# A softcapped attention and mixer kernel: when token weights are decoded, when sums are gathered, and what the start issues first

## The chip, the cores and the metric

The kernel runs on one core of one Trainium2 chip. The metric is device time in microseconds (us) of one execution; below it is called the time. A profiled execution also has a span, from its first to its last instruction.

## The reference

Attention with softcapped scores over 4 batches, 12 heads, 448 positions and 64 columns a head, and then a mixer of two stages with residuals. All is in float32.

```python
scores = (q @ k.T) / sqrt(64)
scores = cap * tanh(scores / cap)
attn = softmax(scores)
x = (attn @ v)                       # heads side by side: 4 x 448 x 768
h = relu(x.T @ w_tok1) @ w_tok2      # over positions: 448 -> 256 -> 448
u = x + h.T
out = u + relu(u @ w_ch1) @ w_ch2    # over columns: 768 -> 1536 -> 768
```

The four weight matrices come as 64-bit floats; the kernel reads their bits and splits each into a high and a low float32 part itself. That is the decode below.

## The kernel before, in words

**Units and steps.** Heads go in pairs (p = 0 to 5 in a batch b), and keys in chunks: three full ones of 128 (c = 0 to 2) and the last 64 keys of two neighbouring pairs packed together (c = 3, which belongs to the even pair). A unit is one (b, p, c). The list of 84 units goes pair 0: c = 0, 1, 2, 3, pair 1: c = 0, 1, 2, pair 2 and so on; a step takes two units, so there are 42 steps (L487), and the units of batch 0 lie in steps 0 to 10.

**What a step does.** A unit's scores are made by `qk_unit` (L173) on TensorE, then `tanh_unit` (L190) and `exp_unit` (L195) on ScalarE write a tile `e`. Step t first multiplies step t's exp tiles with V on TensorE (`pv_full`, `pv_packed`), then calls `scores_of(t + 2)` (L470), which makes scores, tanh and exp two steps ahead and, when a pair's last scores are made, loads the pair three ahead. Then VectorE adds up the exp tiles of step t (`add_up`, L229; `add_packed`, L249), which later gives the softmax's row sums. At the end, `background` (L413) fills TensorE with work of the token mixer that is ready, up to a budget in ns: transposes (L320), `tok1` (L341), `tok2` (L363) and `add_rows` (L256).

**Buffers.** There are 8 tiles `e` (L191); a tile comes free when its PV products and its additions are done. There are two banks for scores (`ps_a`), two for PV outputs (`ps_b`), and two for everything else (`ps_c`). A pair's PV output stays in its `ps_b` bank until `evac` (L274) copies it out on VectorE, which is put at the head of the step after the pair's last product. Pair 2's output is finished in step 5 and copied at the head of step 6; the first product of pair 4 (step 7) takes its bank. Pairs' raw Q and K have three buffers, decode inputs (`wraw`) and decode work tiles (`wz`) two each.

**The order.** The whole attention part is in an order written out by hand (L449): each of the five engines, SP's queue of DMA issues among them, runs its instructions in the order in which the program emits them. `at(d, f, y)` (L71) puts f off by d steps into phase y: phase 0 at the head of a step, before its PV products, phase 1 after `scores_of`, before the additions, phase 2 after `background`, at the end.

**The decode.** `decode` (L88) issues the load of one piece on SP, and then makes seven operations on VectorE in four parts: `first` (L98, L101), `second` (L106, L107), `third` (L110, L111), `fourth` (L115), with one subtraction on GpSimd at the end (L118). The token weights are four pieces, two of 512 and two of 448 columns. A piece is issued in a step that holds a unit with c = 1 of batch 0: steps 0, 2, 4 and 6. `first` comes two steps later at the head, `second`, `third` and `fourth` three, four and five steps later at the end.

**The normalisation.** After the second pair of two has its last chunk, `add_rows` multiplies the added-up tiles with ones in the next step's background. One step on, `take` (L265) copies the sums out on VectorE in phase 1. One step on, in phase 0, `gather` (L279) issues four small DMAs on SP that bring the sums into one tile of 128 partitions. One step on, in phase 1, `norm` (L286) takes the reciprocal on VectorE and stores it. One step on, `spread` (L293) issues four broadcasting loads, and at the end of the step after that `scale_pair` (L299) multiplies the two outputs. Only scaled pairs are transposed, and `tok1` needs the transposes of three pairs.

**The start.** `load_pair(0, 0)` issues Q on SP (L161) and K on ScalarE's queue (L162); the cap follows K (L453); then come pair 1, V, pair 2 and two more V on SP. From the cap VectorE makes the scales of tanh and exp (L463 to L465).

**After the attention** the channel mixer runs, with `tok` work of the last batches as filling; the change touches there only the moment of the last gathers (`pace` is 2 there).

Of the kernel before, what the change touches and what calls it, by code (L numbers as in the profile page):

```python
# [8 lines left out]
F32 = mybir.dt.float32  # L9
# [6 lines left out]
P = 128  # L16
# [14 lines left out]
HALF = C // 2  # L31
NHALF = NC // 2
SP = 32
FREE = 40.0
EPS = 1e-9


@with_exitstack
def tile_softcap_mixer(ctx, tc, qk, v, cap, w1, w2, wc1, wc2, out):
    nc = tc.nc  # L40
# [5 lines left out]
    ps_c = ctx.enter_context(tc.tile_pool(name="ps_c", bufs=2, space=PSUM))  # L46

    def bits(ap):
        return ap.bitcast(F32)

    cap_sb = const.tile([P, 1], F32, name="cap_sb")
# [19 lines left out]
    def at(d, f, y=0):  # L71
        later.setdefault((now[0] + d, y), []).append(f)

    def run(y):
        for f in later.pop((now[0], y), []):
            f()

    def tick(most=3):
        now[0] += 1
        for y in range(most):  # L80
            run(y)
# [4 lines left out]
    pace = [1]  # L86

    def decode(src, n, hi, lo, early, blank):  # L88
        r = wp.tile([P, 2 * DU], I32, tag="wraw", name="wraw")[:, :2 * n]
        nc.sync.dma_start(r, src.bitcast(I32))  # L90
        r = r.rearrange("p (n t) -> p n t", t=2)

        z = wp.tile([P, DU], I32, tag="wz", name="wz")[:, :n]
        zf = bits(z)

        def first():
            if early:
                nc.vector.tensor_scalar(  # L98
                    z, r[:, :, 1], 1, 1, op0=ALU.logical_shift_left, op1=ALU.logical_shift_right
                )  # L100
                nc.vector.tensor_scalar_mul(zf, zf, 2.0 ** -16)  # L101
                return
            nc.scalar.activation(zf, bits(r[:, :, 1]), AF.Abs, scale=2.0 ** -16)  # L103

        def second():
            nc.vector.tensor_scalar(zf, zf, 2.0 ** -31, 2.0 - 2.0 ** -23, op0=ALU.max, op1=ALU.min)  # L106
            nc.vector.tensor_scalar(z, z, 4, 1, op0=ALU.logical_shift_left, op1=ALU.logical_shift_right)  # L107

        def third():
            nc.vector.scalar_tensor_tensor(z, r[:, :, 1], -(1 << 31), z, op0=ALU.bitwise_and, op1=ALU.bitwise_or)  # L110
            nc.vector.scalar_tensor_tensor(z, r[:, :, 0], 29, z, op0=ALU.logical_shift_right, op1=ALU.bitwise_or)  # L111

        def fourth():
            if early:
                nc.vector.tensor_copy(hi, zf)  # L115
            else:
                nc.scalar.activation(hi, zf, AF.Copy)  # L117
            nc.gpsimd.tensor_tensor(lo, zf, hi, op=ALU.subtract)  # L118
            if blank is not None:
                nc.gpsimd.memset(bits(blank), 0.0)  # L120

        d = lag[0]
        at(d, first)
        d += slow[0]
        at(d, second, 2)
        at(d + 1, third, 2)
        at(d + 2, fourth, 2)

    def decode_steps(src, dst, n, early=False, blank=None):
        hi = dst[:, 0].rearrange("p a b -> p (a b)")  # L130
        lo = dst[:, 1].rearrange("p a b -> p (a b)")
        return [
            lambda i=i: decode(
                src[:, i:i + n], n, hi[:, i:i + n], lo[:, i:i + n], early, blank if i + n == hi.shape[1] else None
            )
            for i in range(0, hi.shape[1], n)
        ]
# [20 lines left out]
    def load_pair(b, p):  # L158
        raw = pi.tile([P, 2, S], F32, tag="qkraw", name="qkraw", bufs=3)
        if b == 0 and p == 0:  # L160
            nc.sync.dma_start(raw[:, 0], qk[b, p, :, 0])  # L161
            nc.scalar.dma_start(raw[:, 1], qk[b, p, :, 1])  # L162
        else:
            nc.sync.dma_start(raw, qk[b, p])
        raws[b, p] = raw

    def load_v(b, p):
        nc.sync.dma_start(vn[p % 3], v[b, p])
# [42 lines left out]
    def pv_full(b, p, c):  # L211
        ps, first, last = pv_bank(b, p)
        for j in range(2):
            nc.tensor.matmul(  # L214
                ps[j * D:(j + 1) * D, :S], vn[p % 3][:, j * NF + c], es[b, p, c][:, j], start=first, stop=last
            )

    def pv_packed(b, p):
        for i in range(2):
            ps, first, last = pv_bank(b, p + i)  # L220
            for j in range(2):
                r = half(i, j)
                nc.tensor.matmul(  # L223
                    ps[j * D:(j + 1) * D, :S], vn[(p + i) % 3][r, NV - 1], es[b, p, NF][r, i], start=first, stop=last
                )
# [30 lines left out]
    def add_rows(b, q):  # L256
        ps = ps_c.tile([P, 512], F32, tag="c", name="ps_s")
        acc = accs.pop((b, q))
        for i in range(2):
            for j in range(2):  # L260
                r = (2 * i + j) * SP
                nc.tensor.matmul(ps[r:r + SP, :S], ones, acc[:, i, j], start=True, stop=True, tile_position=(0, r))  # L262
        yield 750, True

        def take():  # L265
            x = px.tile([P, S], F32, tag="xs", name="xs", bufs=1)
            nc.vector.tensor_copy(x, ps[:, :S])
            at(pace[0], lambda: gather(b, q, x))

        read_at(b, None, take)  # L270

# [7 lines left out]
    def gather(b, q, x):  # L279
        s = px.tile([P, S // SP], F32, tag="sums", name="sums", bufs=1)  # L280
        for i in range(4):
            r = slice(i * SP, (i + 1) * SP)
            nc.sync.dma_start(s[r], x[i * SP:i * SP + 1, :].rearrange("p (a c) -> p a c", a=SP))
        at(pace[0], lambda: norm(b, q, s), 1)

    def norm(b, q, s):  # L286
        nc.vector.reciprocal(s, s)
        r = pd.tile([4, S], F32, tag="rs", name="rs")
        nc.sync.dma_start(r.rearrange("h (a c) -> (h a) c", a=SP), s)
        for i in range(2):  # L290
            at(pace[0], lambda i=i: spread(b, 2 * q + i, r[2 * i:2 * i + 2]))
# [104 lines left out]
    second = {}  # L396
# [4 lines left out]
    def read_at(b, f, g):  # L401
        def free():
            unread[0] -= 1
            left[b] -= 1

        if f is not None:
            at(1, f)
        at(1, g, 1)
        at(slack[0], free, 0 if slack[0] > 1 else 1)
# [18 lines left out]
    def split_tile(b, pool):  # L428
        t = last_u if pool is None else pool.tile([P, 2 * NC * S], F32R, name=f"uhl{b}", bufs=1)
        uhl[b] = t.rearrange("p (x c s) -> p x c s", x=2, c=NC)  # L430
# [13 lines left out]
    for m, (b, p, c) in enumerate(units):  # L444
# [5 lines left out]
        engines={engines.PE, engines.DVE, engines.Activation, engines.Pool, engines.SP}  # L450
    ))
    load_pair(*pairs[0])
    nc.scalar.dma_start(cap_sb, cap)  # L453
    nc.vector.memset(near, 0.0)
    nc.scalar.activation(near, near, AF.Exp)
    load_pair(*pairs[1])
# [10 lines left out]
    tokw_steps = decode_steps(w1, w1s, DU, True, w1s[:LAST, 1, NK - 1]) + decode_steps(w2, w2s, S, True)  # L467
# [19 lines left out]
    for t in range(steps_in):  # L487
        two = units[2 * t:2 * t + 2]
        tick(0)
        run(0)  # L490
        for b, p, c in two:
            if c < NF:
                pv_full(b, p, c)
        for b, p, c in two:
            if c == NF:
                pv_packed(b, p)
        scores_of(t + 2)
        run(1)
        for b, p, c in two:
            add_up(b, p, c)  # L500
            n = pairs.index((b, p))
            if c == (2 if p % 2 else NF) and n + 3 < len(pairs):
                at(1, lambda n=n: load_v(*pairs[n + 3]))
            if b == 0 and c == 1 and tokw_steps:
                tokw_steps.pop(0)()
            if b >= 1 and p % 2 and c == 2 and w0_steps:
                w0_steps.pop(0)()
        late = t + 2 - steps_in
        if late >= 0:
            if late == 0:  # L510
                nc.vector.tensor_scalar(
                    mag, cap_sb.bitcast(I32), 1, 1, op0=ALU.logical_shift_left, op1=ALU.logical_shift_right
                )
                in_att.close()
                m0 = ctx.enter_context(tc.tile_pool(name="m0", bufs=1, reuse_waits="tile", side="right"))
                split_tile(0, m0)
            for cc in range(3 * late, 3 * late + 3):
                split_u(0, cc)
        background(TOK / 9)
        run(2)  # L520
        for b, p, c in two:
            if p % NHALF == NHALF - 1 and c == 2:
                work.extend(tok_work(b, p // NHALF))
# [102 lines left out]
    def attend(b, h, vr):  # L626
# [5 lines left out]
        for c in range(NK):  # L632
# [7 lines left out]
            nc.vector.reduce_sum(st[:, 1:2], t, axis=mybir.AxisListType.X)  # L640
            nc.vector.tensor_scalar_add(st[:, 1:2], st[:, 1:2], EPS)
            nc.vector.reciprocal(st[:, 1:2], st[:, 1:2])
# [103 lines left out]
```

## Time and profile before

| | us |
|---|---|
| Runs of the kernel, three | 609.04, 608.09, 607.51 |
| Median of the runs | 608.09 |
| Time of the profiled execution | 606.1 |
| Its span | 604.3 |

The profiled execution is 1.8 us longer than its span: that lies before the first and after the last instruction. Times in the rows below are from the span's start. PE is TensorE's matmul, DVE is VectorE, ACT is ScalarE, POOL is GpSimd, SP is SyncE, and a q behind an engine's name means its queue, which waits or issues a DMA. What stands in square brackets is the idle time of the engine before the row and what ended it. In the rows below L191 and the like are lines of the kernel before.

### The profile page before, as it was taken

How to read it: one execution, taken by the hardware profiler on the slowest of the kernel's cores; microseconds unless marked ns; L12 is line 12 of the kernel's file. 1: busy time of each engine (PE TensorE's matmuls, PEld its weight loads, DVE VectorE, ACT ScalarE, POOL GpSimd, SP SyncE). 2: the span in 40 equal slices, each digit the busy share in tenths (PEclk: the TensorE clock that was granted, in tenths of full speed). 3: DMA queues.
4: the chain of work that ended last, by engine and by line, in shares of the span. 5: the costliest groups of instructions: out<-in, count | busy, mean ns of one | idle time of the engine just before them, and what ended most of it. 6: DMA issues, size and time to landing. Idle time of an engine off the chain costs nothing.

```text
span 604.3 us, 7751 instructions
## 1 busy us (share of the span) xinstructions
PE 590.4 (98%) x3008; PEld 437.3 (72%) x3008; DVE 385.3 (64%) x626; ACT 254.4 (42%) x330; POOL 54.5 (9%) x48
## 2 busy tenths in 40 slices
PE   7998999999999999999999999999999999999997
PEld 2232444444444489997998999899989999999986
DVE  2899869696996996547788386438643853333324
ACT  6998987887879733115332022012211220000000
POOL 0020000000010000002331022001200120000000
PEclk9999999999999999999999999999999999999999
DMA  6445445254442211001344121202120200000224
GB/s 202 149 143 152 143 132 160 78 157 143 130 160 82 68 31 32 0 1 36 96 120 132 36 68 57 86 0 78 63 70 1 69 2 0 1 1 0 94 100 178
DMA packets 24476, 49.12 MB, mean 81 GB/s; under 512 B 6768, under 2 KB 16368, under 8 KB 24432
## 3 DMA queue, kind: packets, MB, share of 16 engines
q1 hardware_dynamic: 24000, 48.21, 24.8%
q8 instruction: 25, 0.41, 0.3%
q10 hardware_dynamic: 432, 0.34, 0.2%
q14 instruction: 19, 0.16, 0.1%
HBM read 42.86 MB, written 5.59 MB: 80 GB/s over the span
## 4 chain that ended last, share of the span: by engine, by line
PE 82%; DVE 10%; ACT 3%; DMA 2%; issue 2%; POOL 0%; DVEq 0%; ACTq 0%; SPq 0%
PE ps_o L563 26%; PE ps_g L546 26%; PE ps_pv L214 8%; PE ps_qk L179 7%; PE ps_h L350 5%; PE ps_u L370 5%; PE ps_s L262 2%; PE ps_pv L223 2%; DMA wraw<-in_wc 1%; DVE wz L110 1%; PE ps_qk L185 1%; PE ps_t L323 1%; ACT e L192 1%; DVE u L568 1%; DVE acc L254 1%
## 5 line engine op out<-in xcount | busy, mean ns | idle before, releaser
L563 PE MATMUL ps_o<-g,wc 128*128 128x448 f32 x864 | 182.8, 367 | 0.2 <-DVE u L568 0.2
L563 PEld LDWEIGHTS ps_o<-g,wc 128*128 128x128 f32 x864 | 161.5, 188 | 15.6 <-DVE u L568 1.3
L546 PE MATMUL ps_g<-uhl,wc 128*128 128x448 f32 x648 | 138.3, 367 | 0.0
L546 PEld LDWEIGHTS ps_g<-uhl,wc 128*128 128x128 f32 x648 | 120.9, 188 | 10.3
L568 DVE TENSOR_TENSOR u<-u,ps_o 128x448 f32<-128x448 f32 (+1 forms) x145 | 86.8, 613 | 47.1 <-PE ps_o L563 46.8
L192 ACT ACTIVATE e<-ps_qk,tsc 128x896 f32<-128x896 f32 x84 | 81.1, 1023 | 28.3 <-PE ps_qk L179 22.3
L197 ACT ACTIVATE e<-e,near 128x896 f32<-128x896 f32 x84 | 83.6, 1059 | 0.0
L118 POOL TENSOR_TENSOR wc<-wz,wc 128x512 fp32r<-128x512 f32 x36 | 48.2, 1342 | 385.6 <-ACT wc L117 364.3
L551 ACT ACTIVATE g<-ps_g 128x896 fp32r<-128x896 f32 x24 | 22.0, 916 | 143.1 <-PE ps_g L546 143.1
L552 DVE SCALAR_TENSOR_TENSOR g<-ps_g,g 128x896 fp32r<-128x896 f32 x24 | 26.1, 1089 | 75.0 <-ACT g L551 75.0
L179 PE MATMUL ps_qk<-qkraw 64*128 64x448 f32 x288 | 67.6, 581 | 4.5 <-DMA qkraw<-in_qk 4.0
L214 PE MATMUL ps_pv<-e,vn 128*64 128x448 f32 x288 | 64.2, 556 | 0.4 <-ACT e L192 0.4
L179 PEld LDWEIGHTS ps_qk<-qkraw 64*128 64x128 f32 x288 | 24.4, 189 | 46.3 <-issue 13.2
L117 ACT ACTIVATE wc<-wz 128x512 fp32r<-128x512 f32 x36 | 22.6, 629 | 74.9 <-PE ps_g L546 33.9
L546 PE MATMUL ps_g<-last_u,wc 128*128 128x448 f32 x216 | 45.5, 367 | 0.7 <-PE ps_o L563 0.6
L546 PEld LDWEIGHTS ps_g<-last_u,wc 128*128 128x128 f32 x216 | 40.4, 188 | 4.8 <-issue 0.9
L103 ACT ACTIVATE wz<-wraw 128x512 f32<-128x512 f32 x36 | 24.2, 673 | 45.8 <-DMA wraw<-in_wc 30.5
L214 PEld LDWEIGHTS ps_pv<-e,vn 128*64 128x64 f32 x288 | 16.5, 135 | 33.3 <-issue 16.0
L106 DVE TENSOR_SCALAR wz<-wz 128x512 f32<-128x512 f32 (+1 forms) x40 | 17.5, 437 | 34.7 <-ACT wz L103 34.6
L350 PEld LDWEIGHTS ps_h<-wc,last_u 128*128 128x128 f32 x176 | 30.5, 188 | 8.0 <-issue 6.0
L350 PE MATMUL ps_h<-wc,last_u 128*128 128x384 f32 x176 | 36.0, 343 | 0.0
L370 PE MATMUL ps_u<-last_u,wc 128*128 128x448 f32 x144 | 34.1, 376 | 1.5 <-DVE wc L359 0.8
(48 smaller groups left out, 410.5 us busy)
## 6 DMA issues: line engine op xcount, KB each, us to landing
wraw<-in_wc SPq DMA_DIRECT2D x36, 512.0 KB, 3.5
qkraw<-in_qk SPq DMA_DIRECT2D x23, 448.0 KB, 3.4
vn<-in_v SPq DMA_DIRECT2D x24, 224.0 KB, 3.3
rb<-rs SPq DMA_DIRECT2D x48, 112.0 KB, 2.8
out_t<-u SPq DMA_DIRECT2D x23, 224.0 KB, 1.9
wraw<-in_w SPq DMA_DIRECT2D x2, 512.0 KB, 4.7
wraw<-in_w SPq DMA_DIRECT2D x2, 448.0 KB, 3.4
sums<-xs SPq DMA_DIRECT2D x48, 1.8 KB, 2.1
```

What stands on the lines that cost most here:

```text
L103: nc.scalar.activation(zf, bits(r[:, :, 1]), AF.Abs, scale=2.0 ** -16)
L118: nc.gpsimd.tensor_tensor(lo, zf, hi, op=ALU.subtract)
L179: nc.tensor.matmul(ps[:, j, :S], raw[r, 1, c * P:(c + 1) * P], raw[r, 0], start=True, stop=True)
L192: nc.scalar.activation(e, scores.pop((b, p, c))[:, :, :S], AF.Tanh, scale=tsc)
L197: nc.scalar.activation(e, e, AF.Exp, scale=near)
L214: nc.tensor.matmul(ps[j * D:(j + 1) * D, :S], vn[p % 3][:, j * NF + c], es[b, p, c][:, j], start=first, stop=last)
L350: nc.tensor.matmul(ps[:, :HALF], w, x, start=(n == 0), stop=(n == len(mm) - 1))
L370: nc.tensor.matmul(ps[:, :S], h1[:, hi, t, cs], w2s[:, wi, t, :], start=(n == 0), stop=(n == 3 * NT - 1))
L546: nc.tensor.matmul(ps[:, i, :S], w[:, wi, cc, fs], uhl[b][:, ui, cc, :], start=(n == 0), stop=(n == 3 * NC - 1))
L552: nc.vector.scalar_tensor_tensor(g[:, 1], ps[:, :, :S], 0.0, g[:, 0], op0=ALU.max, op1=ALU.subtract)
L563: nc.tensor.matmul(ps[:, :S], w[:, wi, i, cs], g[:, gi, i, :], start=(n == 0), stop=(n == 3 * GF - 1))
L568: nc.vector.tensor_tensor(u[b][:, cc, r], u[b][:, cc, r], ps[:, r], op=ALU.add)
```

## The change

- The token-weight pieces are issued one a step, in steps 0 to 3, no longer in steps 0, 2, 4 and 6; and for these pieces all four parts of the decode come together at the end of the step two later (phase 2), so at the ends of steps 2, 3, 4 and 5.
- `gather` is put at the end (phase 2) of the step of the copy, not at the head of the next step; the steps behind it keep their distances and so come one step sooner. Where `pace` is 2, it comes at the end of the next step rather than at the head of the one after.
- At the start, Q goes on SP as before, the first 128 columns of K on ScalarE's queue, then the cap and the other 320 columns of K on SP, ahead of pair 1.
- Two matmuls with zeros, 128 by 384 in float32, are put on TensorE ahead of the first scores; they write a bank of `ps_c` that nobody reads.

```diff
--- before.py
+++ after.py
@@ -33,6 +33,7 @@
 SP = 32
 FREE = 40.0
 EPS = 1e-9
+WARM = 2
 
 
 @with_exitstack
@@ -119,6 +120,10 @@
             if blank is not None:
                 nc.gpsimd.memset(bits(blank), 0.0)
 
+        if early:
+            for f in first, second, third, fourth:
+                at(2, f, 2)
+            return
         d = lag[0]
         at(d, first)
         d += slow[0]
@@ -159,7 +164,9 @@
         raw = pi.tile([P, 2, S], F32, tag="qkraw", name="qkraw", bufs=3)
         if b == 0 and p == 0:
             nc.sync.dma_start(raw[:, 0], qk[b, p, :, 0])
-            nc.scalar.dma_start(raw[:, 1], qk[b, p, :, 1])
+            nc.scalar.dma_start(raw[:, 1, :P], qk[b, p, :, 1, :P])
+            nc.sync.dma_start(cap_sb, cap)
+            nc.sync.dma_start(raw[:, 1, P:], qk[b, p, :, 1, P:])
         else:
             nc.sync.dma_start(raw, qk[b, p])
         raws[b, p] = raw
@@ -265,7 +272,7 @@
         def take():
             x = px.tile([P, S], F32, tag="xs", name="xs", bufs=1)
             nc.vector.tensor_copy(x, ps[:, :S])
-            at(pace[0], lambda: gather(b, q, x))
+            at(pace[0] - 1, lambda: gather(b, q, x), 2)
 
         read_at(b, None, take)
 
@@ -450,7 +457,10 @@
         engines={engines.PE, engines.DVE, engines.Activation, engines.Pool, engines.SP}
     ))
     load_pair(*pairs[0])
-    nc.scalar.dma_start(cap_sb, cap)
+    idle = ps_c.tile([P, 512], F32, tag="c", name="idle")
+    zeros = nc.const_aps.tensor(0.0, [P, HALF], F32)
+    for _ in range(WARM):
+        nc.tensor.matmul(idle[:, :HALF], zeros[:, :P], zeros, start=True, stop=True)
     nc.vector.memset(near, 0.0)
     nc.scalar.activation(near, near, AF.Exp)
     load_pair(*pairs[1])
@@ -501,10 +511,10 @@
             n = pairs.index((b, p))
             if c == (2 if p % 2 else NF) and n + 3 < len(pairs):
                 at(1, lambda n=n: load_v(*pairs[n + 3]))
-            if b == 0 and c == 1 and tokw_steps:
-                tokw_steps.pop(0)()
             if b >= 1 and p % 2 and c == 2 and w0_steps:
                 w0_steps.pop(0)()
+        if tokw_steps:
+            tokw_steps.pop(0)()
         late = t + 2 - steps_in
         if late >= 0:
             if late == 0:
```

## Rows read from the trace of the kernel before

**Rows 1.** The page, busy time of each engine, share of the span, instructions

```profile
PE 590.4 (98%) x3008; PEld 437.3 (72%) x3008; DVE 385.3 (64%) x626; ACT 254.4 (42%) x330; POOL 54.5 (9%) x48
```

**Rows 2.** The windows view: us, busy time by engine, granted clock, DMA share, GB/s

```profile
35.00:40.00 5.00, 5.00 (x34) 1.52 (x32) 4.81 (x9) 5.00 (x7) 0.00 (x0) 1.00 0.27 92
```

**Rows 3.** The timeline of ScalarE: start us, us, engine, line, operation, count, idle before

```profile
6.76 1.91 ACT L192 ACTIVATE e<-ps_qk,tsc 128x896 f32<-128x896 f32 x2 [3.60 <-DVE near L465]
...
50.53 2.00 ACT L192 ACTIVATE e<-ps_qk,tsc 128x896 f32<-128x896 f32 x2
...
56.90 1.91 ACT L192 ACTIVATE e<-ps_qk,tsc 128x896 f32<-128x896 f32 x2 [1.52 <-PE ps_qk L179]
```

**Rows 4.** The timeline of TensorE, steps 7 to 10

```profile
35.90 1.72 PE L214 MATMUL ps_pv<-e,vn 128*64 128x448 f32 x8
...
39.25 0.96 PE L262 MATMUL ps_s<-acc,ones 128*32 128x448 f32 x8
...
53.14 1.10 PE L323 MATMUL ps_t<-ident,u 128*128 128x128 f32 x8 [1.87 <-DVE u L300]
```

**Rows 5.** The timeline, the first normalisation: copy, gather, reciprocal, scaling

```profile
28.98 0.62 DVE L267 COPY xs<-ps_s 128x448 f32<-128x448 f32 x1 [1.11 <-PE ps_s L262]
...
29.63 2.50 SPq L283 DMA_DIRECT2D sums<-xs  x4
...
39.49 0.23 DVE L287 RECIPROCAL sums<-sums 128x14 f32<-128x14 f32 x1
...
52.38 1.15 DVE L300 TENSOR_TENSOR u<-xr,rb 128x448 f32<-128x448 f32 x2
```

**Rows 6.** The timeline of the first 9 us

```profile
1.19 0.46 ACTq L453 DMA_DIRECT2D cap_sb<-in_cap  x1
...
4.01 3.34 PE L179 MATMUL ps_qk<-qkraw 64*128 64x448 f32 x8 [4.01 <-DMA qkraw<-in_qk]
...
6.31 0.16 DVE L463 RECIPROCAL tsc<-cap_sb 128x1 f32<-128x1 f32 x1 [5.44 <-DMA cap_sb<-in_cap]
...
7.82 1.02 PE L179 MATMUL ps_qk<-qkraw 64*128 64x448 f32 x4 [0.47 <-ACT e L192]
```

**Rows 7.** DMA issues of the first 20 us: count, KB each, us to landing

```profile
qkraw<-in_qk ACTq DMA_DIRECT2D x1, 224.0 KB, 3.2
qkraw<-in_qk SPq DMA_DIRECT2D x1, 224.0 KB, 3.0
cap_sb<-in_cap ACTq DMA_DIRECT2D x1, 0.5 KB, 5.1
```

**Rows 8.** The page, DMA issues of the whole run

```profile
sums<-xs SPq DMA_DIRECT2D x48, 1.8 KB, 2.1
```

**Rows 9.** The timeline of VectorE: additions and decode operations

```profile
17.87 1.09 DVE L236 TENSOR_TENSOR acc<-e 128x896 f32<-128x896 f32 x1 [0.67 <-ACT e L197]
19.00 1.25 DVE L254 TENSOR_TENSOR acc<-acc,e 64x448 f32<-64x448 f32 x2
...
21.61 0.42 DVE L106 TENSOR_SCALAR wz<-wz 128x512 f32<-128x512 f32 x1
22.06 0.43 DVE L107 TENSOR_SCALAR wz<-wz 128x512 int32<-128x512 int32 x1
...
26.46 0.68 DVE L110 SCALAR_TENSOR_TENSOR wz<-wraw,wz 128x512 int32<-128x512 int32 x1
27.18 0.69 DVE L111 SCALAR_TENSOR_TENSOR wz<-wraw,wz 128x512 int32<-128x512 int32 x1
...
30.79 0.43 DVE L115 CAST last_u<-wz 128x512 fp32r<-128x512 f32 x1
31.13 0.42 DVE L106 TENSOR_SCALAR wz<-wz 128x512 f32<-128x512 f32 x1
```

**Rows 10.** The timeline, a subtraction of GpSimd over an addition of VectorE

```profile
115.25 1.27 POOL L118 TENSOR_TENSOR wc<-wz,wc 128x512 fp32r<-128x512 f32 x1 [20.52 <-ACT wc L117]
...
116.06 1.41 DVE L236 TENSOR_TENSOR acc<-e 128x896 f32<-128x896 f32 x1
```

## The prediction, made before the changed kernel was run

> **What bounds the kernel now.** I read the engine line first. TensorE is busy 98% of the span [rows 1], so what leaves its work as it is can only pay where TensorE stands still, and can only cost by making it stand still more. All the edits lie in the first 55 us, so I read those. There two other engines are full: ScalarE 5.00 us of 5.00 and VectorE 4.81 [rows 2]. ScalarE sets the pace up to score step 12: its pairs of tanh start at 6.76 and, twelve steps later, at 50.53, which is 3.65 us a step, and only step 13 comes late, at 56.90 after waiting for TensorE [rows 3]. VectorE falls behind it: the scaling that ends the first normalisation comes at 52.38, and TensorE waits 1.87 us for it [rows 4, 5]. So three quantities matter: when ScalarE starts, how late VectorE runs, and what TensorE and ScalarE need from VectorE.
>
> **The start.** The first tanh waits for the cap, not for scores: the cap is issued at 1.19 and used at 6.31, and ScalarE starts 0.45 us later, while TensorE has had its data since 4.01 [rows 3, 6]. The cap took 5.1 us to land, the first Q load 3.0 and K 3.2 [rows 7]. Put behind Q on SP, the cap is issued at about 1.2; if it lands as Q does it is there at 4.2, and tanh could begin at 4.7. The first score unit needs Q and 128 columns of K, which I put at 3.6 (less data than the 4.01 of now), and four matmuls, 1.0 us at the later rate [rows 6] and twice that at the first rate. I take ScalarE's start as 5.0, a gain of 1.8. Ends: no gain, if the cap still takes 5.1; 2.4, if it lands like the small gathers, 2.1 [rows 8], and the first scores are the bound. Two more SP issues of about 0.46, the cap's own on ScalarE's queue [rows 6], stand ahead of the second pair's load and of V; their first users come after 7 us, so I cost them at nothing, and at 0.9 if that cover is gone.
>
> **The zeros.** Two fp32 products of 384 columns are four records; at the first rate, eight records of 448 took 3.34 us in four side-by-side pairs, 0.84 each [rows 6], so four in a row cost 2.9 by their columns, from about 0.8 to 3.7. TensorE stands idle then [rows 6]. Cost zero; if they overrun, some tenths at the first scores.
>
> **The decode.** Number a step by t. Before, four token-weight pieces are issued in steps 0, 2, 4, 6, and VectorE's seven operations for a piece are spread over four steps. After, they are issued in steps 0 to 3, and all seven come in one block at the ends of steps 2, 3, 4 and 5. One block of 512 columns: four scalar operations 0.45 apart, two combinations 0.72 apart, a cast 0.35 [rows 9], together 3.6; for 448 columns 3.6 x 448/512 = 3.2. Four blocks are 13.6 us of VectorE in four steps of 3.65 us, which already hold some 2 us each of other work. Before, only about 6 us of decode stood ahead of step 6; now all of it does.
>
> GpSimd's subtraction follows each cast. Where one overlapped an addition of VectorE, the addition took 1.41 instead of 1.09: of 0.46 us of overlap 0.32, or 0.7, was lost [rows 9, 10]. I use 0.7. The Trainium skill (SBUF — State Buffer, "Who interferes with whom") calls the shared port an exclusive lock under which the second instruction fully blocks; by that the four overlaps below would cost 0.9 us more in all, an estimate, and the measured addition speaks for a little less.
>
> Walk VectorE in its order, with a copy or eviction at 0.6 as the sums' copy [rows 5]. The addition of step 2 starts when its exp ends: 17.87 now [rows 9], 16.1 with the earlier start.
> - Step 2: additions 2.4, block one 3.6: 22.1.
> - Step 3: addition 1.1 + 0.9 (0.7 x 1.27 [rows 10]), block two 3.6: 27.7.
> - Step 4: eviction 0.6, additions 2.15 + 0.5, block three 3.2: 34.2.
> - Step 5: copy of sums 0.6, additions 1.25 + 0.4, block four 3.2: 39.6.
> - Step 6: eviction of pair 2's output 0.6: 40.2.
>
> That eviction frees the accumulator bank (there are two) into which step 7's first PV product goes. TensorE now starts that product at 35.90 [rows 4]; after, at 40.2, 4.3 us later. The same lag holds the exp tiles: step 9's tanh takes tiles that step 6's additions release. VectorE's step 6 goes on with a reciprocal 0.2, additions 3.4 and 0.4 for GpSimd: 44.2. TensorE would be at the row sums of pairs 2 and 3 by 40.2 + 3.4 = 43.6, and needs those additions, so it passes there at 44.2 against 39.25 now [rows 4]: **5.0 us behind**. This contains the start's gain.
>
> **What comes back.** After step 6 VectorE is free of decode. Steps 7 and 8 take it 1.7 and 2.95, so the first scaling (1.2) is done at 50.0. TensorE reaches the transposes at 45.1 + 2 x 3.65 = 52.4 and no longer waits the 1.9 us [rows 4]. Left: 5.0 - 1.9 = 3.1.
>
> **The sums.** The gather is put at the end of the step that copies the sums instead of at the head of the next; on SP nothing lies between, and in the trace the gather goes out at 29.63, as the copy ends (28.98 + 0.62) [rows 5]. So the four DMAs hardly move. What moves is the reciprocal, one whole step, with the store, the broadcast and the scaling behind it. For the first group it came ten microseconds after the gather [rows 5], so there is room. For the second it is close: on SP a pair load stands ahead, which the scores of step 8 release at 45.1 + 3.4 = 48.5; then 0.5 for it, four issues of 0.63 [rows 5] and a landing of 2.1 [rows 8] give 53.5 or so, and VectorE would be there at 50.6. That is a new wait of up to 2.9 us, with the additions of step 9 and the subtractions after the transposes behind it. Ends: nothing, as TensorE needs those only steps later, and 2.9. I take 1.0, nearer to nothing. In later steps TensorE sets the pace, and scaling a step sooner only makes work ready behind work that is queued: zero.
>
> Sum: +3.1 + 1.0 = **+4.1 us**. The profiled execution takes 606.1 us (span 604.3 and 1.8 around it): 610.2. The median of the runs shown, 608.09, is 2.0 above that execution, so I state 612.2.
>
> **Rivals.**
> - *The lag is absorbed* (faster). ScalarE never waited through step 12 [rows 3] while VectorE lagged some 5 us, so buffers hide that much. If they hide the new lag too, the start's 1.8 and the wait of 1.9 are both won: 606.1 - 3.7 = 602.4, or 604.4 in the runs. It decides where pair 2's eviction ends: before 35.9 - 1.8 = 34.1 it wins, and my walk says 40.2. Chance 0.13.
> - *No loss to GpSimd* (no change). If the four overlaps cost nothing, VectorE is 2.2 us sooner and the reciprocal's wait is off the path: 4.1 - 2.2 - 1.0 = +0.9, 609.0. The addition of [rows 10] speaks against it. Chance 0.15.
> - *TensorE slows after the stall* (slower still). TensorE would stand idle from about 36 to 40.2, twice its longest later wait [rows 4]. Its first eight matmuls after the idle start took 3.34 us, later eight 1.72, and by 7.82 the faster rate was there [rows 4, 6]. If the stall brings the slow rate back for the 3.8 us that it lasted at the start, half of them, 1.9, is lost: 614.1. The Trainium skill (TensorE: Matmul & The Clock Gate, Part 1) has such a rule: an idle array falls to the lower of two clocks, 1.2 GHz, and activity lifts it; no row of this kernel shows a fall after the start. Chance 0.15.
> - *The gather is not sooner*: argued above, it is inside every case.
>
> **The numbers.** My forecast has 0.57. About 0.3%, 1.8 us, is what a measurement of this kernel can tell from no change. Faster 0.13, within 0.15, slower 0.57 + 0.15 = 0.72. The range runs from 607.0, which takes in the no-loss case with a better start and leaves out the faster one, to 616.5: no gain at the start is +1.8, the full wait of the reciprocal +1.9, the slower TensorE +1.9, and any two of them on the forecast reach 616.0. Some 0.18 lies outside.
>
> **What would show it.** Right: tanh starts near 5.0; seven decode operations in unbroken blocks on VectorE; TensorE waiting 3 to 5 us near 36 to 41 us for the eviction, ScalarE for additions; the first scaling near 49, no TensorE wait at the transposes; a reciprocal waiting for its gather near 51. Wrong: tanh starts that keep 3.65 us through step 12, or an eviction of pair 2 before 36 us. A cap landing later than 5.5 would break the start alone.

## The result, and the profile after

The changed kernel takes 613.38 us (median of 6 runs, 612.96 to 615.1) against 608.17 us for the kernel before on the same chip (6 runs): a ratio of 1.0088, 95% interval 1.0073 to 1.0102. It is slower by 5.2 us, in the range forecast and 1.2 us above the number forecast. Its profiled execution took 613.69 us with a span of 611.9.

The page's engine line of the changed kernel, which answers to [rows 1], and its row of the granted clock over 40 slices of 15.3 us each:

```profile
PE 596.1 (97%) x3012; PEld 439.7 (72%) x3012; DVE 384.6 (63%) x626; ACT 254.9 (42%) x330; POOL 54.9 (9%) x48
...
PEclk9989999999999999999999999999999999999999
```

TensorE has four records more, the zeros, which are 2.9 us of its 5.7 us of extra busy time. The rest is not new work: it is old work done more slowly, which the 8 in the third slice (30.6 to 45.9 us) already hints at.

The start, as the timeline of the changed kernel has it; it answers to [rows 3, 6]:

```profile
0.78 2.90 PE L463 MATMUL idle<-const-float32-0.0 128*128 128x384 f32 x4 [0.78 <-PEq L745]
...
3.61 4.00 PE L186 MATMUL ps_qk<-qkraw 64*128 64x448 f32 x12
...
3.64 0.17 DVE L473 RECIPROCAL tsc<-cap_sb 128x1 f32<-128x1 f32 x1 [2.76 <-DMA cap_sb<-in_cap]
...
5.53 1.99 ACT L199 ACTIVATE e<-ps_qk,tsc 128x896 f32<-128x896 f32 x2 [2.85 <-PE ps_qk L186]
```

And the first issues of the DMA view (count, KB each, us to landing), against [rows 7]:

```profile
qkraw<-in_qk SPq DMA_DIRECT2D x1, 224.0 KB, 2.5
...
cap_sb<-in_cap SPq DMA_DIRECT2D x1, 0.5 KB, 2.4
```

The cap lands in 2.4 us instead of 5.1, and ScalarE now waits for scores, not for the cap. Its first tanh is 1.23 us sooner.

What follows is lost on VectorE. Its timeline in the changed kernel, from the end of the first decode block to the end of step 6's additions; it answers to [rows 5, 9]:

```profile
22.64 1.08 DVE L249 TENSOR_TENSOR acc<-acc,e 128x896 f32<-128x896 f32 x1
23.64 1.50 DVE L99 TENSOR_SCALAR wz<-wraw 128x512 int32<-128x512 int32 x1
...
28.38 0.62 DVE L283 COPY xr<-ps_pv 128x448 f32<-128x448 f32 x1
28.92 1.85 DVE L243 TENSOR_TENSOR acc<-e 128x896 f32<-128x896 f32 x1
...
35.21 0.62 DVE L274 COPY xs<-ps_s 128x448 f32<-128x448 f32 x1
35.75 1.88 DVE L261 TENSOR_TENSOR acc<-acc,e 64x448 f32<-64x448 f32 x2
37.66 0.40 DVE L99 TENSOR_SCALAR wz<-wraw 128x448 int32<-128x448 int32 x1
...
40.70 0.39 DVE L116 CAST last_u<-wz 128x448 fp32r<-128x448 f32 x1
41.01 0.62 DVE L283 COPY xr<-ps_pv 128x448 f32<-128x448 f32 x1
41.54 0.23 DVE L294 RECIPROCAL sums<-sums 128x14 f32<-128x14 f32 x1
41.69 1.56 DVE L243 TENSOR_TENSOR acc<-e 128x896 f32<-128x896 f32 x1
...
44.64 1.09 DVE L249 TENSOR_TENSOR acc<-acc,e 128x896 f32<-128x896 f32 x1
```

From 22.64 to 45.73 VectorE hardly stands still (what the rows above leave out follows without a gap), and the decode blocks lie in it as unbroken runs (L99 to L116). Pair 2's eviction, the copy from `ps_pv` at 41.01, ends at 41.63.

TensorE's timeline over the same time, against [rows 4]:

```profile
29.10 0.97 PE L221 MATMUL ps_pv<-e,vn 128*64 128x448 f32 x4 [1.35 <-ACT e L199]
...
35.23 0.98 PE L192 MATMUL ps_qk<-qkraw 64*64 64x448 f32 x8
41.72 3.26 PE L221 MATMUL ps_pv<-e,vn 128*64 128x448 f32 x8 [5.51 <-issue]
44.91 2.67 PE L186 MATMUL ps_qk<-qkraw 64*128 64x448 f32 x8
47.52 0.96 PE L269 MATMUL ps_s<-acc,ones 128*32 128x448 f32 x8
...
55.28 1.09 PE L330 MATMUL ps_t<-ident,u 128*128 128x128 f32 x8
```

Step 7's PV product stands 5.51 us and starts 0.09 us after the eviction's end. The view calls the releaser "issue": nothing that it shows was waited for. The reader finds it only by laying the two engines' rows side by side. Behind the wait two groups run at half speed: 3.26 us where the same product takes 1.72 elsewhere, and 2.67 where the scores take 1.77. The windows view says why (columns as in [rows 2]; the bounds are the end of TensorE's work, the fall and the rise of the clock, and a later point):

```profile
36.20:39.95 3.75, 0.01 (x2) 0.00 (x0) 3.57 (x7) 3.20 (x4) 0.32 (x1) 1.00 0.13 22
39.95:46.77 6.82, 5.05 (x14) 1.91 (x16) 6.60 (x11) 0.00 (x0) 1.13 (x1) 0.50 0.39 139
46.77:55.00 8.23, 8.23 (x49) 2.51 (x46) 5.05 (x8) 7.47 (x9) 0.00 (x0) 1.00 0.32 103
```

The granted clock is 1.00 until 39.95, 0.50 (the lower level, 1.2 GHz) from there to 46.77, and 1.00 again. TensorE had been idle for 3.75 us when it fell. In the profiled execution of the kernel before the clock stands at 1.00 from 7.21 to the end. The rows of ScalarE show the same hole, a wait of 7.42:

```profile
35.65 1.90 ACT L199 ACTIVATE e<-ps_qk,tsc 128x896 f32<-128x896 f32 x2
46.82 1.90 ACT L199 ACTIVATE e<-ps_qk,tsc 128x896 f32<-128x896 f32 x2 [7.42 <-PE ps_qk L186]
```

**How far behind.** The row sums come at 47.52 against 39.25 [rows 4], 8.3 us behind. Then some comes back: no wait stands ahead of the transposes at 55.28, where there was one of 1.87 [rows 4], and step 14's tanh is 5.7 behind (67.0 against 61.3). By the first product of the channel mixer it is 7.3 (220.5 against 213.1), and the spans differ by 7.6. The medians differ by less, 5.2: the execution that was profiled before is 2.1 below its median (606.1 against 608.17), the one after 0.3 above. So the traces overstate the loss by some 2 us.

### The profile page after: what moved, and what is told of

Its sections match the earlier page's. It is cut to its first block, busy times and chain, and to the rows that moved or that the text cites. A ratio compares the mean times of both kernels' runs of the same rounds, so it can differ in the third digit from the quotient of the medians.

```text
span 611.9 us, 7769 instructions
## 1 busy us (share of the span) xinstructions
PE 596.1 (97%) x3012; PEld 439.7 (72%) x3012; DVE 384.6 (63%) x626; ACT 254.9 (42%) x330; POOL 54.9 (9%) x48
## 4 chain that ended last, share of the span: by engine, by line
PE 85%; ACT 7%; DVE 4%; issue 2%; DMA 1%; POOL 0%; SPq 0%; DVEq 0%; ACTq 0%; POOLq 0%
PE ps_g L556 27%; PE ps_o L573 27%; PE ps_qk L186 8%; PE ps_pv L221 7%; PE ps_u L377 5%; PE ps_h L357 5%; ACT e L199 3%; ACT e L204 3%; PE ps_s L269 2%; PE ps_pv L230 1%; PE ps_t L330 1%; PE ps_qk L192 1%; DMA wraw<-in_wc 1%; DMA sums<-xs 1%; PE idle L463 0%
## 5 line engine op out<-in xcount | busy, mean ns | idle before, releaser
L221 PE MATMUL ps_pv<-e,vn 128*64 128x448 f32 x288 | 65.5, 567 | 6.9 <-issue 5.5
L186 PEld LDWEIGHTS ps_qk<-qkraw 64*128 64x128 f32 x288 | 24.8, 192 | 43.7 <-issue 15.3
L118 ACT ACTIVATE wc<-wz 128x512 fp32r<-128x512 f32 x36 | 22.6, 628 | 74.7 <-PE ps_g L556 33.9
L377 PE MATMUL ps_u<-last_u,wc 128*128 128x448 f32 x144 | 34.1, 375 | 2.5 <-ACT e L199 1.0
```

Of the source, the lines that this page charges most:

```text
L186: nc.tensor.matmul(ps[:, j, :S], raw[r, 1, c * P:(c + 1) * P], raw[r, 0], start=True, stop=True)
L221: nc.tensor.matmul(ps[j * D:(j + 1) * D, :S], vn[p % 3][:, j * NF + c], es[b, p, c][:, j], start=first, stop=last)
L377: nc.tensor.matmul(ps[:, :S], h1[:, hi, t, cs], w2s[:, wi, t, :], start=(n == 0), stop=(n == 3 * NT - 1))
```

## The experiments

The theory: VectorE's four decode blocks hold pair 2's PV bank and the exp tiles, TensorE stands, and the clock falls while it stands. The main rival: the bank alone, or the gather, or nothing but the clock. First each part was tried alone (the first four), then the theory's links. All were timed with the kernel before on the same chip; its medians there were 607.97 (first four), 608.03 (next four) and 608.09 (last two).

| Run | us, median | ratio, 95% interval |
|---|---|---|
| e1, start alone | 606.52 | 0.9989 (0.9968 to 1.0010) |
| e2, decode alone | 614.00 | 1.0114 (1.0097 to 1.0131) |
| e3, gather alone | 609.07 | 1.0036 (1.0023 to 1.0049) |
| e4, start and gather | 609.09 | 1.0024 (1.0011 to 1.0037) |
| e5, changed kernel, TensorE kept busy in the stall | 612.67 | 1.0077 (1.0054 to 1.0100) |
| e6, changed kernel, pair 2 evicted sooner | 614.36 | 1.0105 (1.0065 to 1.0144) |
| e7, start, second weight's decode late | 604.50 | 0.9941 (0.9924 to 0.9958) |
| e8, changed kernel, second weight's decode late | 610.26 | 1.0040 (1.0024 to 1.0056) |
| e9, as e7 without zeros | 604.92 | 0.9944 (0.9930 to 0.9958) |
| e10, as e7 with the sooner gather | 605.94 | 0.9955 (0.9939 to 0.9970) |

**e1, the start alone.** The kernel before with the edits to `load_pair`, the cap and the zeros:

```diff
-            nc.scalar.dma_start(raw[:, 1], qk[b, p, :, 1])
+            nc.scalar.dma_start(raw[:, 1, :P], qk[b, p, :, 1, :P])
+            nc.sync.dma_start(cap_sb, cap)
+            nc.sync.dma_start(raw[:, 1, P:], qk[b, p, :, 1, P:])
...
-    nc.scalar.dma_start(cap_sb, cap)
+    idle = ps_c.tile([P, 512], F32, tag="c", name="idle")
+    zeros = nc.const_aps.tensor(0.0, [P, HALF], F32)
+    for _ in range(WARM):
+        nc.tensor.matmul(idle[:, :HALF], zeros[:, :P], zeros, start=True, stop=True)
```

> Only the start of the change (Q, part of K, cap and rest of K in the new order, zeros on TensorE); decode and gather as before. Theory (the loss comes from VectorE's decode blocks): the first tanh starts near 5.5 as in the changed kernel, 1.2 us sooner than before, tanh keeps 3.65 us a step through step 12, and the time is 1.2 us below that of before, 606.4 to 607.6. Rival (the new order of loads or the zeros cost what was lost): 609 or more.

Measured: 606.52. The first tanh is at 4.97, but from the second on ScalarE is only some 0.9 us sooner, and so is the first channel product (212.3 against 213.1). TensorE still waits 1.87 us for the first scaling. The gain in the medians, 1.4 us, lies in the range expected, but its interval does not leave out no change, so the sign is not settled by the runs.

**e2, the decode alone.** The kernel before with the two edits to the decode:

```diff
+        if early:
+            for f in first, second, third, fourth:
+                at(2, f, 2)
+            return
...
-            if b == 0 and c == 1 and tokw_steps:
-                tokw_steps.pop(0)()
...
+        if tokw_steps:
+            tokw_steps.pop(0)()
```

> Only the decode of the change (pieces issued in steps 0 to 3, each decoded in one block two steps later); start and gather as before. Theory: the whole loss is here, 5.2 + 1.2 = 6.4 us over the time of before, 613.5 to 615.5, with TensorE idle 4 to 6 us before the first PV product of step 7 and a granted clock of 0.5 for some us behind it. Rival (decode and gather cost only together, through the reciprocal that waits): under 611.

Measured: 614.00, 6.0 us above the kernel before, so the decode alone costs all that the change loses and more. TensorE's timeline of it shows both waits of the changed kernel, and both slow groups:

```profile
30.30 0.97 PE L218 MATMUL ps_pv<-e,vn 128*64 128x448 f32 x4 [1.34 <-ACT e L196]
...
42.94 3.25 PE L218 MATMUL ps_pv<-e,vn 128*64 128x448 f32 x8 [5.52 <-issue]
46.12 2.94 PE L183 MATMUL ps_qk<-qkraw 64*128 64x448 f32 x8
```

The clock is at 0.50 from 41.69 to 48.52.

**e3, the gather alone.** One line of the kernel before:

```diff
-            at(pace[0], lambda: gather(b, q, x))
+            at(pace[0] - 1, lambda: gather(b, q, x), 2)
```

> Only the gather of the change (registered at the end of the step of the copy); start and decode as before. Theory: the four gathers leave SP when they did, the first scaling comes one step sooner in the program, VectorE's reciprocal of the second group waits up to 2 us, and the time stays within 1 us of before, 607.2 to 609.2. Rival (the waiting reciprocal is what costs): 610 to 611.

Measured: 609.07, 1.1 us above, with an interval that leaves out no change. The first scaling is indeed sooner (47.94 instead of 52.38), yet that gains little: TensorE still waits for it, now 1.50 us. The loss lies later. By the windows view TensorE is busy 236.14 of the 240 us from 60 to 300 us, against 237.09 before: 0.95 us less. The view of waits between 100 and 200 us (total us, times, longest), before and then e3, says where:

```profile
PE ps_t L323 <- DVE wc L337: 0.9, 2, 0.7
PE ps_u L370 <- DVE wc L337: 0.3, 1, 0.3
PE ps_u L370 <- ACT wz L103: 0.3, 1, 0.3
```

```profile
PE ps_u L370 <- ACT e L192: 1.0, 1, 1.0
PE ps_t L323 <- DVE wc L337: 0.9, 2, 0.7
PE ps_u L370 <- DVE wc L337: 0.5, 2, 0.3
```

A product of the token mixer's second stage (L370) stands 1.0 us, once, at 195.61, which it did not before. The same wait, 0.96 or 0.97, stands in all seven kernels that gather sooner (in the changed kernel at 200.50), and in none of the five that do not (the kernel before, e1, e2, e7 and e9).

**e4, start and gather.** The changed kernel with the decode as it was before.

> The changed kernel with the decode of before: start and gather changed. Theory: 1.2 us below before, within 1 us, 606 to 608; no granted clock under 1.0 after the start, no wait of TensorE over 2 us. Rival (the gather's waits cost whatever the decode does): 610 or more.

Measured: 609.09. In the profiled execution the clock stands at 1.00 throughout from 4.07, and there is no wait near 36 us: without the decode blocks the stall does not come. (Three of the ten executions have a mean granted clock of 0.996 or 0.997; the last section has more on that.) The time came above what was expected, level with e3: beside the sooner gather the start's gain does not show in the medians, though e4's trace is 1.0 us ahead of e3's at the first channel product (214.5 against 215.5).

**e5, the clock alone.** The changed kernel with seven zero products, which nothing reads, ahead of step 7's first PV product:

```diff
+        if t == 7:
+            hold = ps_c.tile([P, 512], F32, tag="c", name="hold")
+            for _ in range(7):
+                nc.tensor.matmul(hold[:, :HALF], zeros[:, :P], zeros, start=True, stop=True)
```

> The changed kernel with seven zero products (128 by 384, float32) on TensorE just ahead of step 7's first PV product, where it stands idle from 36.1 to 41.7; nothing reads them. Theory: they fill some 4.5 us of the idle time, the granted clock stays 1.0, the PV and score products of step 7 take 3.4 us instead of 5.9, and the row sums behind them start when VectorE's additions end, near 45.7 instead of 47.5: 1.8 us less than the changed kernel, 611 to 612.2. Rival (the lower clock was covered by VectorE's lag, or zeros don't hold it): 613 to 614.

TensorE's timeline of it:

```profile
36.08 4.81 PE L504 MATMUL hold<-const-float32-0.0 128*128 128x384 f32 x14
41.66 1.72 PE L221 MATMUL ps_pv<-e,vn 128*64 128x448 f32 x8 [0.78 <-issue]
43.31 1.77 PE L186 MATMUL ps_qk<-qkraw 64*128 64x448 f32 x8
45.02 1.65 PE L269 MATMUL ps_s<-acc,ones 128*32 128x448 f32 x8
```

The product still starts at 41.66, when VectorE lets it, but at full rate, and the clock is 1.00 throughout from 4.76. The row sums come at 45.02 instead of 47.52, and from there every step is 1.8 us sooner than in the changed kernel (first channel product 218.6 against 220.5). That the fall of the clock costs 1.8 us at that place is shown. What it costs the whole kernel is not: the profiled spans differ by 1.3 and the medians by 0.7, with intervals that overlap, and the time came just above what was expected.

**e6, the bank alone.** In the changed kernel pair 2's eviction is put ahead of the fourth decode block:

```diff
-            at(1, lambda: evac(b, p))
+            if (b, p) == (0, 2):
+                later.setdefault((now[0], 2), []).insert(0, lambda: evac(b, p))
+            else:
+                at(1, lambda: evac(b, p))
```

> The changed kernel with one edit: pair 2's output is copied out of its bank at the end of step 5, ahead of the fourth decode block, not behind it. Theory (the lag itself is the cause, the bank only its first claimant): step 7's first PV product starts near 38.5 instead of 41.7, but tanh of step 9 and the row sums of pairs 2 and 3 still wait for step 6's additions until 45 or so; 0 to 2 us less than the changed kernel, 611.3 to 613.4. Rival (the bank alone is the cause): 4 us or more less, 609.4 or under.

TensorE's timeline of it:

```profile
38.51 2.97 PE L224 MATMUL ps_pv<-e,vn 128*64 128x448 f32 x8 [2.17 <-ACT e L199]
...
43.52 0.95 PE L272 MATMUL ps_s<-acc,ones 128*32 128x448 f32 x4
46.31 0.94 PE L272 MATMUL ps_s<-acc,ones 128*32 128x448 f32 x4 [1.85 <-DVE acc L252]
```

The product starts 3.2 us sooner, 0.10 after the eviction's end (38.41), and little comes of it: the trace is 1.2 us ahead at the first channel product (219.2 against 220.5), and the median, 614.36 from four runs, is no lower than the changed kernel's and above what was expected. The second half of the row sums waits for VectorE's additions until 46.31, and the clock falls all the same, from 38.85 to 42.27. The bank is where the lag shows first, not its cause; free it, and the next thing that VectorE owes is late.

**e7, the load taken off.** The start part with the decode spread as before, and the second weight's two pieces issued in steps 9 and 11 instead of 4 and 6:

```diff
-            if b == 0 and c == 1 and tokw_steps:
-                tokw_steps.pop(0)()
...
+        if tokw_steps and t in (0, 2, 9, 11):
+            tokw_steps.pop(0)()
```

> The start of the change, the gather of before, and the decode spread as before but with the two pieces of the second token weight issued in steps 9 and 11 instead of 4 and 6 (they are first read near 95 us). Theory: without these two pieces VectorE is some 4 us less behind at the first scaling, TensorE's wait of 1.9 us for it goes, and tanh keeps 3.65 us a step through step 12: 1.2 to 2.5 us below the kernel with the start alone (606.5), 604 to 605.3. Rival (the wait is given back in later steps, where the late pieces load VectorE): 606 to 607.

TensorE's timeline of it, and then VectorE's first scaling:

```profile
35.29 1.72 PE L217 MATMUL ps_pv<-e,vn 128*64 128x448 f32 x8
...
49.93 1.10 PE L326 MATMUL ps_t<-ident,u 128*128 128x128 f32 x8
```

```profile
46.32 1.15 DVE L303 TENSOR_TENSOR u<-xr,rb 128x448 f32<-128x448 f32 x2
```

The scaling is done at 47.5, the transposes come 3.2 us sooner than before [rows 4] without a wait, and the kernel takes 604.50, in the range expected: it beats both kernels. Against e1, which has the same start and differs by the late decode alone, it gains 2.0 us, with intervals that do not overlap. Moving decode the other way, out of the first steps, is what pays here.

**e8, half the load.** The changed kernel with `t in (0, 1, 9, 11)` in that line: blocks one and two stay, three and four come late.

> The changed kernel, blocks and all, with the third and fourth piece issued in steps 9 and 11 instead of 2 and 3: two blocks stand ahead of step 6, not four. Theory: VectorE reaches pair 2's eviction 6.4 us and some contention sooner, near 33.5, before TensorE needs the bank; no idle over 2 us, no lower clock, and the time is that of start and gather without the decode (609.1) or a little less, 606.5 to 609. Rival (a block of seven operations costs by its form, whatever stands ahead): 611 or more.

Measured: 610.26, 3.1 below the changed kernel and 1.3 above the upper end expected. Step 7's PV starts at 36.06 without a stall and the clock holds 1.00, so blocks three and four, ahead of step 6, make the stall. Two blocks ahead of it already make TensorE wait once:

```profile
29.03 0.97 PE L221 MATMUL ps_pv<-e,vn 128*64 128x448 f32 x4 [1.35 <-ACT e L199]
...
47.75 1.09 PE L330 MATMUL ps_t<-ident,u 128*128 128x128 f32 x8
...
61.44 0.66 PE L330 MATMUL ps_t<-ident,u 128*128 128x128 f32 x4 [1.31 <-DVE u L307]
```

Pair 1's eviction stands behind block two and ends at 28.93 here, 29.00 in the changed kernel and 30.21 in e2. TensorE's product follows 0.09 or 0.10 us later in each, after a wait of 1.34 or 1.35 that the view puts down to ScalarE. That wait is given back by the first transposes: they come at 47.75 here, and at 47.84 in e4, which has no blocks but waits 1.88 there for the first scaling. What e8 loses against e4 comes later, beside the blocks that were put off. The next scaling stands behind block three, and TensorE waits 1.31 us for it; e4 has a wait of 0.95 shortly before, and e8 is then 0.2 us behind (65.54 against 65.34). The copy of the sums behind that scaling is 0.8 late, and with it a gather, a reciprocal and an addition for which TensorE waits 0.89 us, where e4 waits 0.28. Then an eviction stands behind block four (70.59 to 74.01) and ends at 74.66, and the second half of the packed PV products starts at 74.72. After that e8 is 1.6 behind (77.33 against 75.74). The medians differ by 1.2, with intervals that overlap.

**e9 and e10, parts of e7.** e9 is e7 with `WARM = 0`, e10 is e7 with the line of e3.

> The kernel of the late second weight (604.5) without the zero products ahead of the first scores. Theory (the zeros lift the clock before the data come): the granted clock reaches 1.0 near 7 us instead of 3.7, the first tanh starts 0.5 to 0.9 us later than its 4.9, and the time is 605 to 605.5. Rival (the zeros do nothing for the first scores, which come at the slow rate either way): 604.2 to 604.8.

> The kernel of the late second weight with the gather of the changed kernel. Theory (the sooner reciprocal holds VectorE up in many steps, whatever the decode does): 1 to 2.5 us above 604.5, 605.5 to 607. Rival (it costs only where the decode has put VectorE behind): 604 to 605.

ScalarE's second tanh of e7, and then of e9:

```profile
7.05 1.01 ACT L195 ACTIVATE e<-ps_qk,tsc 128x896 f32<-128x896 f32 x1 [1.16 <-PE ps_qk L182]
```

```profile
7.47 1.01 ACT L195 ACTIVATE e<-ps_qk,tsc 128x896 f32<-128x896 f32 x1 [0.65 <-PE ps_qk L182]
```

Without zeros the clock is at 1.00 only from 9.17, with them from 3.67. The first tanh starts at 5.81 without and 4.88 with them, the second, as shown, 0.4 us apart, and 0.4 us it stays in every later step. The medians differ by 0.4 too, with intervals that overlap: the zeros' worth is not settled, and is small. Over all twelve traces the clock is at 1.00 from 3.67 to 6.45 us with zeros (eight traces) and from 7.21 to 9.17 without (four), but e10, which has them, starts its first tanh at 5.87, no sooner than e9. e10 is 1.4 above e7 in the median, the sign of e3, with the wait of 0.96 there again at 192.75; these intervals overlap as well, so that the gather costs is shown by e3.

The parts in the medians: start -1.4, decode +6.0, gather +1.1, together +5.7; the whole change +5.2. That the sum fits does not make the parts independent: start and gather together cost 1.1 (e4) where their sum is -0.3, and the decode adds 4.3 on top of both (613.38 against 609.09) and 6.0 alone. Why they combine so was not tried.

## Why the prediction was right, and where it was off

The sign, the place and the mechanism were right. Decode blocks fill VectorE from step 2 to step 5, pair 2's eviction comes at 41 us, TensorE stands at step 7's PV, and the changed kernel is slower. Most signs named beforehand came, some later or larger: unbroken blocks of seven operations, TensorE's wait between 36 and 42 (5.5 us, where 3 to 5 were named), no wait at the transposes, a reciprocal that waits for its gather (from 53.25, not near 51). One did not: ScalarE's long wait is for TensorE's scores (7.42), not for additions. Term by term:

- **The start.** The cap lands in 2.4 us, sooner than the 3.0 taken, but the first tanh is at 5.53, not 5.0. The step that was off is the price of the first four matmuls: with data at 3.6, as forecast, the start taken lies between 4.6 at the later rate and 5.6 at the first, and they ran at the first, twelve in 4.00 us. In e1 the fast rate came earlier and the tanh was at 4.97. The zeros cost nothing, as forecast: 0.78 to 3.68.
- **VectorE's walk.** Block one ends at 22.6 (22.1 forecast), block two at 28.4 (27.7), three at 35.2 (34.2), four at 41.0 (39.6). Of the 1.4 us, 0.5 is the later start. Some 0.7 is GpSimd: what VectorE lost in the first three overlaps is 1.07, 0.76 and 0.63 (1.50, 1.85 and 1.88 where 0.43, 1.09 and 1.25 are usual), against 0.9, 0.5 and 0.4. The rest is the seven operations: the first block is as forecast, the two of 448 columns take some 0.15 more each (3.35 for the fourth, 3.2 forecast).
- **The lock.** The 0.7 taken from one row was too low. The rows to lay beside each other are GpSimd's in the changed kernel:

```profile
22.81 2.05 POOL L119 TENSOR_TENSOR last_u<-wz,last_u 128x512 fp32r<-128x512 f32 x1 [21.44 <-DVE last_u L116]
28.55 1.27 POOL L119 TENSOR_TENSOR last_u<-wz,last_u 128x512 fp32r<-128x512 f32 x1 [3.68 <-DVE last_u L116]
...
41.17 1.13 POOL L119 TENSOR_TENSOR last_u<-wz,last_u 128x448 fp32r<-128x448 f32 x1 [4.65 <-DVE last_u L116]
```

  VectorE's addition of 28.92 ends at 30.77, 0.95 after GpSimd's end at 29.82. That of 41.69 ends at 43.25, again 0.95 after (42.30). That of [rows 10] ends at 117.47, once more 0.95 after (116.52). An addition alone takes 1.09. So it is held until GpSimd is done, all but some 0.14 us of it, whatever the overlap. The prediction took the loss as a share of the overlap, which one row could not tell from that. With the fourth (1.56 for 1.09) the four losses come to 2.9 us, where 2.2 was taken. The Trainium skill (SBUF — State Buffer, "Who interferes with whom") has it so: one of the two holds the shared port and the other blocks. By that rule the estimate in the prediction was 0.9 us above the 2.2, and the trace agrees within 0.2. The copies out of PSUM and the reciprocal that overlapped a subtraction kept their usual 0.62 and 0.23.
- **Behind at the row sums.** Forecast 5.0, measured 8.3. The product starts 1.5 later than forecast, the walk's miss. Then PV and scores of step 7 take 5.8 us instead of 3.4, as the clock is at its lower level. The 0.6 that the additions were to add falls away behind that.
- **The clock.** This rival had 0.15 and a price of 1.9; it happened, and e5 puts 1.8 us on it at that place. In the medians 0.7 is left, which is not clear of noise. Its number, 614.1, and the forecast, 612.2, lie on either side of the 613.38 measured. The step that failed is the one that chose between them: "no row of this kernel shows a fall after the start" was taken as evidence against, but the longest wait after the start in that trace is 1.87 us, so it could say little about a stall of four. (The runs timed later show the clock lower in some executions of that kernel too, as the last section says; no trace was at hand of one.) By the rule of the Trainium skill that was quoted ("TensorE: Matmul & The Clock Gate", Part 1), an idle array falls to the lower clock; the trace agrees, 0.50 after 3.75 us idle.
- **What comes back.** The 1.9 at the transposes came back in full. The first scaling ended at 52.7, not 50.0, still ahead of TensorE.
- **The gather.** Put at 1.0 through a reciprocal's wait: that wait was there, 2.52 us at 55.77. But the cost lies elsewhere too. "In later steps ... zero" was wrong: sooner scaling brings a new wait of 0.97 us near 195 to 200 us, in each kernel that gathers sooner. That it is the moved background work is argued from where it stands; which order of it makes the wait was not tried.
- **Missed, at no cost here:** pair 1's eviction behind block two, 1.35 us of TensorE at 29.1. The walk had that eviction in step 4, after block two, and asked only of pair 2's who waits for it. In the changed kernel the wait lies ahead of a longer one that ends when VectorE does, and VectorE had not stood still for it; in e8, where the longer one is gone, it is given back.

Of the rivals, "the lag is absorbed" fell with the eviction at 41.6 where it needed 34.1, and "no loss to GpSimd" fell with the rows above. On the traces the loss is 7.6, not 4.1; that the forecast came within 1.2 us of the median is in part luck, as the execution profiled before was 2 us below its median. Some 0.7 of the 2 us is the clock: over 54 later executions of the kernel before the median is 608.0, over the 32 of them that kept the full clock, as the profiled one did, 607.3. Where the rest lies stays open.

## What to carry to other kernels

When work is pulled together on an in-order engine, walk that engine to its end and ask of every copy behind the block which bank it frees and who wants that bank next. Work that nobody needs soon goes where the engine has room: with the same start, two pieces of the decode put five steps later made this kernel 0.6% faster (e7, 0.9924 to 0.9958), 2.0 us of it beyond the start alone, where the change made it 0.9% slower. Put late in whole blocks (e8) they made TensorE wait beside them, though what that costs is not clear of noise. Where a forecast stall is longer than any idle time that the trace holds, price what follows at the lower clock as well.

## What was not expected of the hardware

- One stall of 5.5 us cost TensorE more than itself: the clock fell to 0.50 after 3.75 us of idleness and stayed there until 46.77, 5.05 us after work had resumed. In e6 it fell too, after a wait of 2.17, where the 1.87 in the trace of the kernel before [rows 4] had left it up. Fourteen zero records in the gap held it at 1.00 (e5).
- The clock is lower for a while in some executions of the kernel before as well. Of the 54 that were timed beside e1 to e10, 22 have a mean granted clock of 0.997 and a median of 608.4 us, the others 0.999 or 1.0 and 607.3. In e6 0.997 is one fall of 3.42 us. Values of 0.996 or 0.997 stand in 9 of the 26 executions of e1, e3 and e4, and in none of the 39 of e5 and e7 to e10. Where the clock fell in those executions no trace here shows; the traces of the first group, at full clock, have a wait of 1.50 to 1.88 us for the first scaling, and those of the second have none there.
- Which of two instructions loses on the shared port goes by which started first. The addition at 22.64 kept its 1.08 and GpSimd's subtraction of 22.81 took 2.05 instead of 1.27; where GpSimd started first, the addition lost. A decode operation with a single tile as input (L99, 1.50 for 0.43) lost as the additions did.
- A load of 128 four-byte pieces landed in 5.1 us behind K on ScalarE's queue [rows 7] and in 2.4 behind Q on SP's. Why was not tried.
